# Turning the second half's rows with VectorE and a round trip through DRAM in a spectral filter plus GEGLU kernel

## Chip, cores and metric

One core of a Trainium2 chip runs the whole kernel. The metric is the device time of one execution in microseconds, median over runs. TensorE (PE), VectorE (DVE), ScalarE (ACT) and GpSimd (POOL) each work through their own list of instructions in order; SyncE (SP) issues DMA transfers from a queue of its own, also in order.

## The reference

```python
def _A_ref(x, w_r, w_i):                      # x: 1 x 2048 x 512
    X = rfft2(x, axes=(-2, -1))
    X = X * (w_r + 1j * w_i)                  # 2048 x 257
    return irfft2(X, s=(S, D), axes=(-2, -1))
def _B_ref(x, w_gate, w_up, w_down):          # 512 -> 1376 -> 512
    return (gelu(x @ w_gate) * (x @ w_up)) @ w_down
h = x + _A_ref(layernorm(x), w_r, w_i)        # layernorm: eps 1e-5, no scale or shift
h2 = h + _B_ref(layernorm(h), w_gate, w_up, w_down)
```

Everything is float32. The gelu is the tanh approximation.

## The kernel before

The rows are 16 blocks of 128 (block b), the 512 columns four chunks of 128. Both Fourier transforms are matrix products. The MLP has 11 blocks f of 128 hidden columns; the rows of blocks 0 to 7 are the first half, 8 to 15 the second, and a **tile** t{n} is one hidden block for one half: t0 to t10 for the first half, t11 to t21 for the second. Every float32 operand of the MLP stands as two parts, a high and a low one (fp32r), and a product of two operands is three matmuls. A tile computes gate and up with seven products P0 to P6 over combinations of the operand's quarters in place of eight; a product is six matmuls of 128x512. The seven combinations of the rows stand in `cb`, those of the weights in `gu`.

The order of work is written out by hand. Strings of tokens (`START`, `SECOND`, `FIRST`, `FIRST_HALF`, `SECOND_HALF`) list steps; each step gives its instructions to its engines in the order of the string. SyncE's transfers and some other things are placed by the scheduler. The strings, in order of time:

- `START`: statistics and roots of layer norm (s, r, n), sums of rows (f, u, v), and for each b the transform over rows (a, b) until some 31 us.
- `SECOND`: over d (o), the filter (f), back (b), with p and h as preparations.
- `FIRST`: the way back of the first eight blocks, their second layer norm, their turning (T) and combinations, and the first tiles.
- `FIRST_HALF`: tiles t2 to t10 and all that makes the second half's rows. Its tokens: t{n}P0 to P6 the products; t{n}c1 to c3 copies by ScalarE out of PSUM; d1, d2, dy the sums of products and m0, m1, o0, o1 the end of a tile, on VectorE; G0, G1 gelu; i0, i1 rounding of the result. y{n}.k is a step on the weights of tile n: raw loads by SyncE, differences by GpSimd, rounding to the high part by ScalarE, low part by GpSimd (t10's are y10). D{g}{i}@k is the down projection of group g of tiles for row block i into PSUM bank k; E{g}{i} adds that bank to `gh` and so gives it back. For the last group D30 and D31 are begun without their last tile, and F30, F31 do that third (three matmuls). N0, N1 are inverse roots of the second half's variances, each two Newton chains of short operations; S0 (`keep_rows`) writes scales and means of the second half's rows to DRAM, for `rescale` and `means` to spread them later.

The part that the change touches most: a normalised row block of 128x512 must stand with its columns on the partitions before TensorE can use it as `cb`. For the second half, `turned(i, banks)` works on block 8 + i (h = 0) and 12 + i (h = 1). H{i}{h} normalises on ScalarE. T0 and T1 transpose four 128x128 pieces each by TensorE against `ident` into a PSUM bank (lines 596 and 602). Then a, b make high and low part of combinations 0 and 1; s, z, e are copies by ScalarE into SBUF; c, d, h, k are the differences, f, g / i, j, n, o / l, m high and low part of the others. All of this comes late in `FIRST_HALF`, after t9's products; i{i}x is step x of pair i. The copies s and z also put the turned rows into `gh` (`ht`), where the second half keeps its residual.

Of the kernel before, what the change touches and what calls it, by code (L numbers as in the profile page):

```python
# [51 lines left out]
u4.0 w4 u0.1 C4.0 w0 C0.1 U1.2 C1.4 U5.3 C5.5 V4.2 X4 V0.3 X0 M4.1 O4.0 V1.0 M0.2 O0.1 X1 r0 V5.1 X5 H4 G4 H0 I4 U2.3  # L52
C2.5 V2.3 M5.1 U7.2 H5 C7.1 S4 O5.0 G0 A4 g0awh I0 S0 A0 M1.3 O1.1 Q0 U3.4 E0.5 V7.4 X2 C3.5 U6.0 C6.0 N0 R01 I5 R00
H1 G5 S5 X7 M2.1 V6.3 H2 G1 I1 S1 X6 U8.4 C8 T01.2 s0.0 O2.1 l0 T00 A5 A1 c0 V3.1 Q1 M7.0 O7.0 E1.6 U9.7 a0 N1 R10
M6.4 T10 X3 I2 d0 e0.1 k0 H7 H6 f0 g0 b0 h0 U12.3 G2 R11 T11.1 a1 I7 M3.2 C12 U15.3 b1 g0aP0 s1.2 c1 i0 G7 O3.1 O6.0
U10.4 n0 H3 d1 j0 S7 C15 C9 e1.0 g1aP0 h1 m0 k1 n1 C10 f1 l1 I3 G3 S3 I6 A7 U14.5 A3 g1 G6 g1aP1 g0ac1 g0aP2 g0aP3 Q3
g0awl g1ac1 g1aP2 C14 o0 E3.7 N3 o1 i1 m1 R31 T31.5 S2 g0ac2 A2 S6 A6 R30 Q2 r1 s3.6 E2.6 N2 j1 g0aP4 T30 c3 g0aP1 d3
g1ac2 g1aP4 g0ac3 g0aP5 R20 T20 g0ad1 a3 b3 e3.4 h3 k3 g1ac3 g1aP5 r2 f3 R21 g0ady g0aP6 g3 g1aP3 i3 j3 T21.7 a2 b2
g0bP0 g0aG0 g1ad1 g1ady K9.5 g0ad2 g0bP1 s2.8 n3 c2 d2 g1bP0 g1aP6 K12.4 g1bP1 g0bc1 g0bd1 r3 l2 f2 g2 g0bP2 g0aG1
g0am1 g1bc1 g1bP2 g1aG0 e2.7 k2 n2 g1ad2 o3 g0bc2 h2 o2 m2 l3 i2 g0am0 g0bG0 g1bd1 g0bP3 g1bc2 g0bP4 g0ai1 g1aG1 j2  # L60
g0bc3 g0bdy g1bP4 g1bP3 g0ai0 g1bc3 g1awh g0bP5 m3 g1am0 g0bP6 K8.4 lo1 g1ai0 g1bdy g1bG0 g1bP6 g0ao0 g1ao0 g0ao1
# [85 lines left out]
def kernel(  # L147
# [508 lines left out]
    def in_turn(i, hns, banks):  # L656

        do = combine(i, hns)
        places = {"T0": ps[:, banks[0]], "T1": ps[:, banks[1]], "s": ht[:, 1, :, i], "z": ht[:, 0, :, i], "e": row()}
        for names in ("T0 a b z", "T1 s c d e f g h k", "i j l m n o"):  # L660
            for k in names.split():
                do[k](*[places[k]] if k in places else [])
            yield
# [782 lines left out]
```

## Time and profile before

| | |
|---|---|
| time, median of 3 runs | 437.88 us (437.83 to 438.65) |
| profiled execution: span from first to last instruction | 436.2 us |
| TensorE busy | 429.6 us (98%), 2283 matmuls |
| VectorE busy | 303.7 us (70%) |
| ScalarE busy | 262.3 us (60%) |
| GpSimd busy | 326.4 us (75%) |
| DMA moved | 41.61 MB, mean 95 GB/s |

The profiled execution has no time of its own beside the span; the median of the runs is 1.7 us above the span, which is what lies before the first and after the last instruction, or between executions. A share of busy time is an average over stages; the rows further down are from single stages. TensorE's granted clock is at its full level, 2.4 GHz, in every slice of the page.

### The profile page before, as it was taken

The page shows a single profiled execution, that of the slowest core. Times are in us where ns is not written, and L with a number is a line of the kernel's source. Part 1 is how long each engine was busy: PE and PEld are TensorE (multiplying, and loading weights), DVE is VectorE, ACT ScalarE, POOL GpSimd, SP SyncE. Part 2 cuts the span into 40 slices and gives each one's busy share as a digit, 9 for nine tenths or more (in the row PEclk, how much of TensorE's full clock was granted, in tenths as well). Part 3 has the DMA queues.
Part 4 walks back from the last instruction along what each step waited for, and adds up shares of the span by engine and source line. Part 5 has one row for each costly group of instructions (what it writes and reads, how often), then busy time and mean ns, then how long its engine had stood idle before and what let it go on. Part 6 is the DMA issues. An engine that isn't in the chain of part 4 may idle for free.

```text
span 436.2 us, 6671 instructions
## 1 busy us (share of the span) xinstructions
PE 429.6 (98%) x2283; PEld 368.6 (84%) x2283; DVE 303.7 (70%) x570; ACT 262.3 (60%) x536; POOL 326.4 (75%) x355
## 2 busy tenths in 40 slices
...
GB/s 286 402 414 85 379 23 144 106 50 24 2 121 122 73 49 98 72 25 72 72 11 63 98 50 120 146 46 28 72 49 73 54 44 57 65 26 0 1 2 194
DMA packets 23543, 41.61 MB, mean 95 GB/s; under 512 B 4178, under 2 KB 9810, under 8 KB 23380
## 3 DMA queue, kind: packets, MB, share of 16 engines
...
q14 instruction: 17, 0.14, 0.1%
...
## 4 chain that ended last, share of the span: by engine, by line
PE 92%; DMA 4%; POOL 1%; DVE 1%; issue 1%; ACT 0%; SPq 0%; DVEq 0%; POOLq 0%
PE ps L192 16%; PE ps L190 16%; PE ps L191 16%; PE ps L1241 14%; PE ps L1034 11%; DMA gh<-in_x 4%; PE ps L454 3%; PE ps L563 3%; PE ps L469 3%; PE ps L496 3%; PE ps L826 2%; PE ps L1212 1%; POOL pn L368 1%; PE ps L1142 1%; PE ps L596 1%; PE ps L602 1%
## 5 line engine op out<-in xcount | busy, mean ns | idle before, releaser
L190 PE MATMUL ps<-cb,gu 128*128 128x512 f32 (+1 forms) x336 | 125.8, 375 | 0.0
L192 PE MATMUL ps<-cb,gu 128*128 128x512 f32 (+1 forms) x336 | 124.9, 372 | 0.0
L191 PE MATMUL ps<-cb,gu 128*128 128x512 f32 (+1 forms) x336 | 124.8, 371 | 0.0
L706 ACT ACTIVATE s<-ps 128x512 f32<-128x512 f32 (+1 forms) x72 | 40.3, 561 | 56.7 <-PE ps L192 56.4
L257 POOL TENSOR_TENSOR gu<-raw,gu 128x768 fp32r<-128x768 f32 (+1 forms) x42 | 61.6, 1483 | 16.7 <-ACT gu L254 14.7
L190 PEld LDWEIGHTS ps<-cb,gu 128*128 128x128 f32 x336 | 63.3, 188 | 11.0 <-ACT s L706 0.2
L192 PEld LDWEIGHTS ps<-cb,gu 128*128 128x128 f32 x336 | 63.2, 188 | 11.0
L191 PEld LDWEIGHTS ps<-cb,gu 128*128 128x128 f32 x336 | 63.3, 188 | 10.9
L1241 PE MATMUL ps<-wd,a 128*128 128x512 f32 x264 | 63.4, 390 | 0.0
L1241 PEld LDWEIGHTS ps<-wd,a 128*128 128x128 f32 x264 | 49.3, 188 | 10.1
L712 ACT ACTIVATE s<-s 128x512 f32<-128x512 f32 (+1 forms) x48 | 28.4, 593 | 33.5 <-DVE s L709 33.3
L715 DVE TENSOR_TENSOR ps<-ps,s 128x512 f32<-128x512 f32 (+1 forms) x48 | 30.9, 651 | 22.5 <-PE ps L192 19.9
L1041 DVE TENSOR_TENSOR gh<-ps,gh 128x512 f32<-128x512 f32 x66 | 44.2, 681 | 0.8 <-PE ps L1034 0.8
L709 DVE TENSOR_TENSOR s<-ps,s 128x512 f32<-128x512 f32 (+1 forms) x48 | 30.7, 641 | 17.2 <-PE ps L192 15.8
L254 ACT ACTIVATE gu<-raw 128x768 fp32r<-128x768 f32 (+1 forms) x42 | 28.6, 698 | 4.9 <-POOL raw L240 4.6
L1253 DVE TENSOR_TENSOR gh<-ps,gh 128x512 f32<-128x512 f32 x24 | 16.4, 686 | 19.8 <-PE ps L1241 19.8
L709 DVE TENSOR_TENSOR ps<-ps,s 128x512 f32<-128x512 f32 (+1 forms) x24 | 15.6, 652 | 17.0 <-ACT s L706 14.5
L544 POOL TENSOR_TENSOR wd<-wdr,wd 128x512 fp32r<-128x512 f32 x12 | 15.5, 1295 | 13.9 <-ACT wd L542 13.9
L234 POOL TENSOR_TENSOR raw<-raw 128x256 f32<-128x256 f32 x16 | 11.8, 737 | 17.2 <-DMA raw<-in_wgu 15.5
L947 POOL TENSOR_TENSOR t<-mis,t 128x768 fp32r<-128x768 f32 (+1 forms) x9 | 13.3, 1481 | 14.1 <-ACT t L945 14.0
L728 DVE TENSOR_TENSOR a<-ps,a 128x512 fp32r<-128x512 f32 (+1 forms) x26 | 15.1, 603 | 10.8 <-ACT a L721 10.5
L485 POOL TENSOR_TENSOR z<-t,t 128x520 f32<-128x520 f32 x15 | 19.4, 1295 | 2.7 <-DVE t L477 2.1
...
## 6 DMA issues: line engine op xcount, KB each, us to landing
...
raw<-in_wgu SPq DMA_DIRECT2D x32, 256.0 KB, 3.1
out<-gh SPq DMA_DIRECT2D x15, 256.0 KB, 2.0
...
row<-in_x SPq DMA_DIRECT2D x12, 256.0 KB, 3.6
wdr<-in_wd SPq DMA_DIRECT2D x12, 256.0 KB, 2.7
mis<-in_wd SPq DMA_DIRECT2D x10, 256.0 KB, 2.6
a<-in_wgu SPq DMA_DIRECT2D x8, 256.0 KB, 3.5
```

The lines of the kernel that those rows point to most:

```text
L190: pe.matmul(o, lh, rh, start=(i == 0 and not onto), stop=False, skip_group_check=True)
L191: pe.matmul(o, lh, rl, start=False, stop=False, skip_group_check=True)
L192: last = pe.matmul(o, ll, rh, start=False, stop=(i == n - 1), skip_group_check=True)
L254: by.activation(r[:, 0, m], t[:, m], AF.Copy)
L257: pooled["lo"] = pool.tensor_tensor(r[:, 1, m], t[:, m], r[:, 0, m].bitcast(F32), op=ALU.subtract)
L706: return lambda: act.activation(to, a, AF.Copy)
L709: return lambda: dve.tensor_tensor(to, a, b, op=ALU.add)
L712: return lambda: act.activation(g, g, AF.Gelu_apprx_tanh)
L715: return lambda: dve.tensor_tensor(u, u, g, op=ALU.mult)
L1034: pe.matmul(ps[:, k], w[:, hw], a[ha], start=start and hw + ha == 0, stop=hw == 1, skip_group_check=True)
L1041: by.tensor_tensor(to, o, to, op=ALU.add)
L1241: pe.matmul(o, a[:, ha, i // 4, rows_of], wds[f][:, hw], start=start, stop=stop)
```

## The change

The 32 TensorE transposes of the second half go. `turned(h)` now lets VectorE transpose each normalised block, 128x512, into a tile `t`: J{i}{h}. VectorE turns pieces of 32x32 only, so the pieces still lie in the wrong partitions. When the four blocks of a half h are there, J{h} (`leave`) writes `t` to DRAM (`across`) in four transfers of 256 KB, one for each 32 partitions, and reads it back into `gh` in one of 1 MB: ten transfers for both halves. `combined(i, banks)` then makes the combinations out of `gh`: s, z, e are not needed, i and j now take two combinations in one step, b and m stand on GpSimd. Rows come out in another order within a half, which is undone when the output is taken apart. `keep_rows` turns scales and means with one small VectorE transpose, too, and writes them with four transfers of rows of 128 bytes, in place of two of single words. In `FIRST_HALF` the tokens of all this stand elsewhere, and `START`, `SECOND` and `FIRST` list the same steps in another order. The matmuls of START, SECOND and FIRST are the same in number.

```diff
 START = """
-f0 s0 g0 r0 n0 s1 c0 v0 g1 s2 m3 q3 r1 g2 f1 v1 n1 r2 m5 c1 q5 n2 c2 m7 c3 f2 s4 s6 g4 a0 b0 w7 g6 v2 q7 r4 n4 m9 c4
...
+s0 g0 r0 n0 s1 c0 m3 q3 f0 v0 g1 s2 r1 g2 r2 m5 f1 n1 v1 c1 q5 n2 c2 c3 f2 v2 s4 s6 g4 g6 m7 q7 r4 n4 a0 b0 w7 m9 c4
...
 FIRST_HALF = """
...
-i0T1 Z0 w9.2 i1z t10c2 t10P4 i0a i0b i0s i0c t10P3 i0d t10d1 t10c3 t10dy i0z i0e i0h Z1 i0f i0g w10.0 w10.1 t10P5 i0i
-E32 D34@6 i1e i1k i2e i2k i1h i2n i3e i2b i3k i3n E33 i2o i1n i1o i3a i3b D35@7 i2f i2h i3m i3h E34 D36@6 i1l i1m i3o
+t7m1 E21 D23@7 E20 D22@6 t8dy t8P6 t7i1 t7o1 H31 J31 H01 J01 E22 t8d2 t9P1 t8G0 H11 J11 H21 J21 t8P5 D24@6 w8.0 E23
+t10i0 t10o0 D31@7 i2h D30@6 F30 E30 i2k t10i1 t10o1 i2f i2g i2i i2j i1h i3c F31 E31 D32@6 i3k E32 D34@6 i3d i3f i1l
+i1g i2l i2m i3h i3i i1k i3j i3g E34 D33@7 D36@6 E33 i1i i1j D35@7 E35 D37@7 i3l i3m i1m i0l E36 i0m E37
...
         def rescale():
             for r in range(2):
-                at = kept_rows[0][4 * r : 4 * r + 4].rearrange("b n -> (b n)")
+                at = kept_rows[r].rearrange("q i n -> (q i n)")
                 spreading = nc.sync.dma_start(spread, at.partition_broadcast(P))
                 if not r:
...
-                nc.sync.dma_start(m[:1], kept_rows[1][4 * k : 4 * k + 4].rearrange("(o b) n -> o (b n)", o=1))
+                nc.sync.dma_start(m[:1], kept_rows[2 + k : 3 + k].rearrange("o q i n -> o (q i n)"))
...
-    kept_rows = [dram.tile([NB // 2, P], F32, name=f"rows{i}") for i in range(2)]
+    kept_rows = dram.tile([4, 4, 4, 32], F32, name="rows")
...
     def keep_rows():
-        sd = w3.tile([P, NB // 2], F32, name="sd", bufs=1)
-        dve.scalar_tensor_tensor(sd, mv2[:, NB // 2 :, 1], EPS, rs2[:, NB // 2 :], op0=ALU.add, op1=ALU.mult)
-        for to, a in zip(kept_rows, (sd, mv[:, NB // 2 :, 0])):
-            nc.sync.dma_start(to.rearrange("b n -> n b"), a)
-    def turned(i, banks):
-        hn = [None, None]
-        def normed(h):
-            hn[h], b = row(), 8 + i + 4 * h
-            act.activation(hn[h], gh[:, b], AF.Copy, scale=rs2[:, b : b + 1])
-        for h in range(2):
-            later[f"H{i}{h}"] = functools.partial(normed, h)
-        ops = combine(i, hn)
-        places = {"T0": ps[:, banks[0]], "T1": ps[:, banks[1]], "s": ht[:, 1, :, i], "z": ht[:, 0, :, i]}
-        for k in "T0 a b z T1 s c d e f g h k i j l m n o".split():
-            if k == "e":
-                later[f"i{i}e"] = lambda: ops["e"](row())
-            elif k in places:
-                later[f"i{i}{k}"] = functools.partial(ops[k], places[k])
-            else:
-                later[f"i{i}{k}"] = ops[k]
+        sd, st = (w3.tile([P, 32], F32, name=n, bufs=1) for n in ("sd", "st"))
+        dve.memset(sd, 0.0)
+        dve.scalar_tensor_tensor(sd[:, :8], mv2[:, NB // 2 :, 1], EPS, rs2[:, NB // 2 :], op0=ALU.add, op1=ALU.mult)
+        dve.tensor_copy(sd[:, 8:16], mv[:, NB // 2 :, 0])
+        dve.transpose(st, sd)
+        for q in range(4):
+            nc.sync.dma_start(kept_rows[:, q].rearrange("k i n -> k i n"), st[32 * q : 32 * q + 16])
+    def turned(h):
+        tr, hns = None, {}
+        def normed(i):
+            hns[i], b = row(), 8 + i + 4 * h
+            act.activation(hns[i], gh[:, b], AF.Copy, scale=rs2[:, b : b + 1])
+        def turn(i):
+            nonlocal tr
+            if tr is None:
+                tr = w3.tile([P, 16, 4, 32], F32, name="t", bufs=1)
+            dve.transpose(tr[:, :, i], hns[i])
+        def leave():
+            for q in range(4):
+                at = slice(32 * q, 32 * q + 32)
+                to = across[h].rearrange("(j r) n -> r j n", r=32)[:, :, q * P : (q + 1) * P]
+                nc.sync.dma_start(to, tr[at].rearrange("r j i n -> r j (i n)"))
+            nc.sync.dma_start(htf[:, h], across[h].rearrange("(c p) n -> p c n", p=P))
+        for i in range(4):
+            later[f"H{i}{h}"] = functools.partial(normed, i)
+            later[f"J{i}{h}"] = functools.partial(turn, i)
+        later[f"J{h}"] = leave
+    def combined(i, banks):
+        hi, lo = cb[:, 0, :, :, i], cb[:, 1, :, :, i]
+        a0, a1, s0, s1 = (ht[:, h, c : c + 2, i] for h in range(2) for c in (0, 2))
+        w = [ps[:, k].rearrange("p (m c n) -> p m c n", m=2, c=2) for k in banks]
+        def less(to, a, b, eng=dve):
+            return lambda: eng.tensor_tensor(to, a, b, op=ALU.subtract)
+        def high(m, a):
+            return lambda: act.activation(hi[:, m], a, AF.Copy)
+        def low(m, a, eng=dve):
+            return lambda: eng.tensor_tensor(lo[:, m], a, hi[:, m].bitcast(F32), op=ALU.subtract)
+        first = ht[:, 0, :, i].rearrange("p (m c) n -> p m c n", c=2)
+        ops = {
+            "a": high(slice(0, 2), first),
+            "b": low(slice(0, 2), first, pool),
+            "c": less(w[0][:, 0], s0, a0),
+            "d": less(w[0][:, 1], s1, w[0][:, 0]),
+            "f": high(slice(3, 5), w[0]),
+            "g": low(slice(3, 5), w[0]),
+            "h": less(w[1][:, 1], a1, w[0][:, 1]),
+            "k": less(w[1][:, 0], s1, s0),
+            "i": high(slice(5, 7), w[1]),
+            "j": low(slice(5, 7), w[1]),
+            "l": high(2, s1),
+            "m": low(2, s1, pool),
+        }
+        for k in ops:
+            later[f"i{i}{k}"] = ops[k]
+    across = [dram.tile([D, 4 * P], F32, name=f"across{h}") for h in range(2)]
+    for h in range(2):
+        turned(h)
...
     for i, banks in enumerate(((3, 4), (5, 0), (3, 4), (1, 2))):
-        turned(i, banks)
+        combined(i, banks)
...
-    y[:, NB // 2 :, ORDER] = second.reshape(D, NB // 2, P).transpose(2, 1, 0)
+    y[:, NB // 2 :, ORDER] = second.reshape(D, 2, 4, 4, 32).transpose(2, 4, 1, 3, 0).reshape(P, NB // 2, D)
```

Three places of the program, as the engines' lists stand in it. The first is SyncE's queue while the second half's rows are made: `raw<-in_wgu` are loads of weights, `rows` and `dis` carry the scales (S0 and the spread of `rescale`), `wdr` the down weights. Before:

```order
L538 DMA wdr<-in_wd 128x512
L1264 DMA rows_925<-sd 128x8x1
L227 DMA raw<-in_wgu 128x512
L228 DMA raw<-in_wgu 128x2x256
L1059 DMA dis<-rows_925 128x512
L538 DMA wdr<-in_wd 128x512
L227 DMA raw<-in_wgu 128x512
```

After, from the load of down weights ahead of S0 on:

```order
L537 DMA wdr<-in_wd 128x512
L1257 DMA rows<-st 4x4x32 x4
L1280 DMA across_926<-t 32x16x128 x4
L226 DMA raw<-in_wgu 128x512
L227 DMA raw<-in_wgu 128x2x256
L1281 DMA gh<-across_926 128x4x512
L1049 DMA dis<-rows 128x512
L1280 DMA across_927<-t 32x16x128 x4
L1281 DMA gh<-across_927 128x4x512
L537 DMA wdr<-in_wd 128x512
```

The one scatter of scales gave way to four transfers; the four writes of the first half h and their reading back stand ahead of the spread `dis<-rows`, those of the second behind it, and so behind the wait of that spread for GpSimd's first step on tile ten's weights.

The second place is TensorE behind tile ten's last product: L1241 and L1231 are the down projection (D30 and so on, nine matmuls each, F30 and F31 three), L596 and L602 the transposes, L190 to L192 and L189 to L191 products of tiles. Before:

```order
L192 MATMUL ps<-cb,gu 128x512
L1241 MATMUL ps<-wd,a 128x512 x12
L602 MATMUL ps<-ident,row 128x128 x4
L1241 MATMUL ps<-wd,a 128x512 x3
L602 MATMUL ps<-ident,row 128x128 x8
L596 MATMUL ps<-ident,row 128x128 x4
L1241 MATMUL ps<-wd,a 128x512 x3
L596 MATMUL ps<-ident,row 128x128 x4
L1241 MATMUL ps<-wd,a 128x512 x54
```

After:

```order
L191 MATMUL ps<-cb,gu 128x512
L1231 MATMUL ps<-wd,a 128x512 x27
L189 MATMUL ps<-cb,gu 128x512
L190 MATMUL ps<-cb,gu 128x512
L191 MATMUL ps<-cb,gu 128x512
...
L190 MATMUL ps<-cb,gu 128x512
L191 MATMUL ps<-cb,gu 128x512
L1231 MATMUL ps<-wd,a 128x512 x18
L189 MATMUL ps<-cb,gu 128x512
L190 MATMUL ps<-cb,gu 128x512
L191 MATMUL ps<-cb,gu 128x512
```

Before, the transposes stood between the pieces of D30 to F31, and then 54 matmuls of down projection came in a row. Now D31, D30 and F30, F31 and D32 are 27 matmuls without a break, and two products of tile eleven, 12 matmuls, stand between D32 and D34.

The third place is VectorE at the same time: L709/L699, L715/L705 and L728/L718 are d2 and m, o and j of tile ten, L1250/L1240 the sums E3i, L618/L1295 the differences c, d, h, k and L624/L1301 the low parts. Before:

```order
L709 TENSOR_TENSOR s_2464<-ps,s_2464 128x512
L715 TENSOR_TENSOR ps<-ps,s_2463 128x512
L715 TENSOR_TENSOR ps<-ps,s_2464 128x512
L728 TENSOR_TENSOR a<-ps,a 128x512
L624 TENSOR_TENSOR cb<-ps,cb 128x4x128
L728 TENSOR_TENSOR a<-ps,a 128x512
L1250 SCALAR_TENSOR_TENSOR gh<-ps,mv,gh 128x512
L618 TENSOR_TENSOR ps<-gh,ps 128x256 x3
L1250 SCALAR_TENSOR_TENSOR gh<-ps,mv,gh 128x512
L618 TENSOR_TENSOR ps<-gh,ps 128x256 x3
L1250 SCALAR_TENSOR_TENSOR gh<-ps,mv,gh 128x512
L618 TENSOR_TENSOR ps<-ps,row 128x256
```

After:

```order
L718 TENSOR_TENSOR a<-ps,a 128x512
L1295 TENSOR_TENSOR ps<-gh,ps 128x256
L1240 SCALAR_TENSOR_TENSOR gh<-ps,mv,gh 128x512
L1295 TENSOR_TENSOR ps<-gh 128x256
L718 TENSOR_TENSOR a<-ps,a 128x512
L1301 TENSOR_TENSOR cb<-ps,cb 128x4x128 x2
L1295 TENSOR_TENSOR ps<-gh,ps 128x256
L1295 TENSOR_TENSOR ps<-gh 128x256
L1240 SCALAR_TENSOR_TENSOR gh<-ps,mv,gh 128x512
L1295 TENSOR_TENSOR ps<-gh 128x256
L1240 SCALAR_TENSOR_TENSOR gh<-ps,mv,gh 128x512
L1295 TENSOR_TENSOR ps<-gh,ps 128x256
```

The differences now read `gh` and not PSUM banks that TensorE had filled; three of them stand between E30 and the next sums, and the order of sums and low parts is another.

## Rows read from the trace of the kernel before

**Rows 1.** The page: busy time, share of the span and instructions of each engine.

```profile
PE 429.6 (98%) x2283; PEld 368.6 (84%) x2283; DVE 303.7 (70%) x570; ACT 262.3 (60%) x536; POOL 326.4 (75%) x355
```

**Rows 2.** Stretches: us, busy (instructions) of PE, PEld, DVE, ACT, POOL; PEclk, DMA share, GB/s.

```profile
238.00:255.00 17.00, 17.00 (x82) 13.96 (x81) 10.55 (x18) 11.94 (x23) 12.77 (x14) 1.00 0.19 63
255.00:262.00 7.00, 7.00 (x43) 6.00 (x42) 6.34 (x11) 5.62 (x13) 3.33 (x5) 1.00 0.20 76
262.00:274.00 12.00, 12.00 (x55) 9.92 (x54) 10.19 (x21) 5.79 (x17) 5.12 (x8) 1.00 0.34 119
300.00:430.00 130.00, 130.00 (x575) 107.63 (x574) 100.01 (x160) 70.96 (x125) 96.75 (x93) 1.00 0.14 45
```

**Rows 3.** The chain that ended last, pieces of it: start, duration, what.

```profile
220.91 4.08 PE ps L1241 x18
...
245.52 0.44 PE ps L596 x4
...
255.09 2.73 PE ps L1241 x12
...
258.26 0.70 PE ps L1241 x3
258.95 0.87 PE ps L602 x8
...
261.39 12.27 PE ps L1241 x54
```

**Rows 4.** Timeline of VectorE: start, duration, line, operation [idle before, releaser].

```profile
215.46 0.16 DVE L576 SCALAR_TENSOR_TENSOR rs<-ps,rs 128x4 f32<-128x4 f32 x1
...
244.19 0.69 DVE L709 TENSOR_TENSOR s<-ps,s 128x512 f32<-128x512 f32 x1 [1.36 <-PE ps L192]
...
262.06 1.09 DVE L618 TENSOR_TENSOR ps<-gh,ps 128x256 f32<-128x256 f32 x3
...
277.09 2.47 DVE L1064 TENSOR_TENSOR gh<-gh,ps 128x512 f32<-128x512 f32 x4
```

**Rows 5.** Groups of VectorE from 240 to 275 us: the sums E3.

```profile
L1250 DVE SCALAR_TENSOR_TENSOR gh<-ps,mv,gh 128x512 f32<-128x512 f32 x8 | 6.0, 750 | 1.8 <-PE ps L1241 1.7
```

**Rows 6.** DMA issues: count, KB each, median us from issue to landing.

```profile
raw<-in_wgu SPq DMA_DIRECT2D x32, 256.0 KB, 3.1
out<-gh SPq DMA_DIRECT2D x15, 256.0 KB, 2.0
...
mis<-in_mi SPq DMA_DIRECT2D x1, 1024.0 KB, 9.5
...
rows<-sd SPq DMA_DIRECT2D x1, 4.0 KB, 10.8
```

**Rows 7.** Timeline of GpSimd, the weights of tile ten.

```profile
233.69 0.74 POOL L234 TENSOR_TENSOR raw<-raw 128x256 f32<-128x256 f32 x1 [11.51 <-DMA raw<-in_wgu]
...
241.51 1.86 POOL L257 TENSOR_TENSOR gu<-raw,gu 128x768 fp32r<-128x768 f32 x1 [0.86 <-ACT gu L254]
```

**Rows 8.** Timeline of ScalarE, tile ten's last rounding and its copy c1.

```profile
240.60 0.84 ACT L254 ACTIVATE gu<-raw 128x768 fp32r<-128x768 f32 x1
...
242.89 0.60 ACT L706 ACTIVATE s<-ps 128x512 f32<-128x512 f32 x1 [1.45 <-PE ps L192]
```

**Rows 9.** Timeline of TensorE and of VectorE near the end of the first stage.

```profile
26.10 0.61 PE L401 MATMUL ps<-ms,uv 128*128 128x128 f32 x4
26.90 0.68 PE L401 MATMUL ps<-ms,us 128*128 128x128 f32 x4 [0.19 <-DVE us L388]
27.42 0.61 PE L401 MATMUL ps<-ms,uv 128*128 128x128 f32 x4
27.87 0.61 PE L401 MATMUL ps<-ms,us 128*128 128x128 f32 x4
...
25.81 1.41 DVE L388 TENSOR_TENSOR us<-pn 128x256 f32<-128x256 f32 x2
```

More of the change, by code (lines that the diff above doesn't have):

```diff
@@ L36 @@
 START = """
-f0 s0 g0 r0 n0 s1 c0 v0 g1 s2 m3 q3 r1 g2 f1 v1 n1 r2 m5 c1 q5 n2 c2 m7 c3 f2 s4 s6 g4 a0 b0 w7 g6 v2 q7 r4 n4 m9 c4
-s8 c5 c6 q9 a1 a2 b1 a3 f4 f6 m11 b2 k0 v4 s10 q11 g10 g8 c7 v6 b3 a4 f8 a5 b5 b4 r8 k2 k1 n8 c8 s12 f10 a6 m13 c9 c10
-c11 k4 a7 b7 f12 f14 q13 s15 v8 g12 s14 k3 b6 k7 g15 a8 a9 k5 g14 r12 v10 n12 b8 v12 b9 k9 c12 a11 u13 c13 a10 b10 u14
-k8 f15 b11 a12 b12 k6 a13 k10 c14 c15 k11 v14 u15 b13 k13 k12 v15 a14 b14 a15 b15 z4 l15 k14 k15
+s0 g0 r0 n0 s1 c0 m3 q3 f0 v0 g1 s2 r1 g2 r2 m5 f1 n1 v1 c1 q5 n2 c2 c3 f2 v2 s4 s6 g4 g6 m7 q7 r4 n4 a0 b0 w7 m9 c4
+s8 c6 c5 q9 a1 b1 a3 f4 f6 m11 b2 k0 v4 s10 q11 g10 c7 v6 g8 r8 k1 a2 k2 n8 c8 b3 a4 f8 a5 b5 b4 s12 f10 a6 m13 c9 k4
+q13 c11 c10 f14 a7 b7 f12 v8 g12 s14 b6 k7 k3 s15 g15 a8 a9 k5 g14 v10 r12 n12 b8 v12 b9 k9 c12 a11 u13 c13 a10 b10
+u14 k8 b11 a12 b12 k6 k11 v14 b13 a13 c14 k10 c15 k12 k13 f15 v15 a14 b14 u15 a15 l15 b15 z4 k14 k15
 """
@@ L51 @@
 FIRST = """
[L52 to L61, printed above, removed]
@@ L84 @@
-L15 t7P3 R15 t7P4 t6d2 y8.4 y8.5 y8.6 y8.7 y8.8 y8.9 y8.10 t7c3 t6o0 t7dy t6G1 t6m1 t8P0 t8c1 B14.1 t7G0 t6i1 B11.1
-t7P5 t7m0 t7i0 t8P2 B15.0 w7.0 y9.0 y9.1 w7.1 t7P6 t8P3 w7.2 y9.2 y9.3 t6o1 t7o0 t8c2 y9.4 y9.5 B15.1 N0 N1 t8P4 t8c3
-H00 H01 H10 t8P1 H11 y9.6 t7d2 t7G1 y9.7 y9.8 y9.9 D21@7 D20@6 t9P0 E21 D23@7 E20 D22@6 S0 t8d1 t8G0 t7m1 t7i1 t7o1
-t9P1 y9.10 y10.0 t8P5 t9c1 t9d1 t9P2 H20 H21 E22 y10.1 t8dy D24@6 t8P6 w8.0 E23 D25@7 y10.2 H30 t8d2 y10.3 E24 D26@6
-t8m0 H31 t8G1 t8m1 y10.4 y10.5 y10.6 y10.7 y10.8 E25 D27@7 t8i0 E27 t9c2 w8.1 w8.2 t9P4 t9G0 t8i1 t9P3 t9c3 w9.0 y10.9
```

46 lines of the change are left out of this document (26 added, 20 removed).

## The prediction

> **What bounds the kernel now.** I read the page's busy line first, then the chain that ended last, then busy time by stretch. TensorE is busy for 429.6 of 436.2 us [rows 1], and in all four stretches that matter here, from 238 us on, it is busy for the whole stretch [rows 2]. The chain of work that ended last is there an unbroken run of matmuls [rows 3]: no other engine releases any of them. So a microsecond of TensorE work taken out is worth a microsecond, as long as TensorE finds its next operands ready. VectorE is the next fullest: 6.3 of 7 us and 10.2 of 12 us in the stretches from 255 to 274 us [rows 2], which is where the change adds VectorE work and takes TensorE work away.
>
> **What is removed.** The second half's rows are turned by 32 TensorE transposes, eight groups of four. One group takes 0.44 us in the chain, a double one 0.87 us [rows 3]: 8 x 0.44 = 3.5 us, all of it on the path. Twelve copies on ScalarE (s, z, e) go too; ScalarE has 5.8 busy us in the 12 from 262 us [rows 2], so they are worth nothing by themselves. **Removed: 3.5 us.**
>
> **The turning by VectorE.** Eight transposes of 128x512, SBUF to SBUF. The trace has none. Below, four back-to-back 128x512 operations take 2.47 us, 0.62 us apiece [rows 4]; above, the dearest row of that size on any engine that could do it is GpSimd's 768-wide one at 1.86 us [rows 7], which for 512 columns is about 1.25 us. I take 0.6 to 0.7 us, since every VectorE row of this width lies there. In the changed order five stand just behind the two chains of short operations on the variances, which ended at 215.6 us [rows 4], before the sums E21 and E20 that give back banks 7 and 6. Behind 215.6 us come the five (3.25 us), tile seven's m1 (0.62 us) and E21 (0.75 us [rows 5]): E21 ends near 220.3 us. Its bank is wanted by D23, which with D22 begins at 220.91 us in the chain [rows 3] and has one product more ahead of it now, 222.3 us. At 1.25 us each, E21 would end near 223.2 us and cost 0.9 us.
>
> The row of TensorE says 0.44 us per 128x512 on an engine without idle time [rows 3]. The Trainium skill, "DVE Perf Modes", section "Rules for kernel authors", speaks against the change: it gives a 128x128 transpose to TensorE wherever PSUM may be its target. By that rule there would be no gain, 437.9 us; by the row there is one, because VectorE's extra 5 us fall into its idle time and TensorE's 3.5 us did not.
>
> **The round trip.** Four writes of 256 KB and one read of 1 MB for each half. For the second: its last two transposes stand behind the sum E22 and tile eight's d2. The chain has D23 and D22 end at 220.91 + 4.08 = 224.99 us [rows 3]; the new order puts one product more ahead of them (1.36 us, six matmuls at 12.27/54 = 0.227 us [rows 3]) and tile eight's P6 after them: 227.7 us, and with d2 and two transposes 229.6 us. SyncE issues the four writes by 231 us. The stated landing of 256 KB is 2.0 us for a store [rows 6]: the four land at 233 us if they overlap, at 239 us if each waits for the last. The read of 1 MB lies between a 256 KB load at 3.1 us and the 1 MB of mis at 9.5 us [rows 6]: back at 236 to 248.5 us, and I take 241 us. The first reader is i1c, on VectorE right behind tile nine's d2, which starts at 244.19 us in the profile [rows 4] and moves by little: 244.9 us. Covered by 4 us in the middle, late by 3.6 us at the worst end. SyncE's queue has the spread of the scales ahead of these writes, waiting for GpSimd's first step on tile ten's weights; that step came at 233.69 us, 11.5 us late, behind the scatter of 4-byte words rows<-sd that took 10.8 us to land [rows 6, 7]. But for that it could have come at 222.2 us. The scatter is gone; I put the step at 227 us, between, and expect no wait for it at 229.6 us.
>
> **Terms that cost.** Let T be the end of tile ten's last product, 255.09 us in the chain [rows 3].
>
> (1) Weights of tile ten. Its last rounding (0.84 us, at 240.60 us [rows 8]) moves on ScalarE behind the copy c1 of the same tile, which starts at 242.89 us [rows 8]. So it ends near 242.89 + 0.60 + 0.84 = 244.33 us, and GpSimd's low half (1.86 us [rows 7]) at 246.2 us. P2 now stands where a transpose group began, at 245.52 us [rows 3], and its third matmul, the first to read the low half, two matmuls later, at 245.97 us: **0.25 us**.
>
> (2) F30. After T the order on VectorE is d2, j of row group 0, m1, o0; m1 waits for a gelu, which I take at the 0.60 us of ScalarE's copy of that width [rows 8]. With steps of 0.6 us on VectorE [rows 4]: d2 to 0.75, j to 1.35, m1 1.45 to 2.05, o0 to 2.75 us. Before, F30 came at 258.26 us, T + 3.17 [rows 3], with a transpose group as filler; now it could start 12 x 0.227 = 2.73 us after T. Nearly even if VectorE is punctual at T, up to 0.4 us if its list from i1c on (in which I count 0.9 us without work, by the same steps) is a little late: 0.2 us.
>
> (3) D32 into bank 6 now has only F31 (0.68 us) between it and F30, which wrote that bank. The sum E30 must come between: it takes 0.75 us [rows 5], and I allow 0.1 us for the handing over. So D32 waits 0.85 - 0.68 = 0.17 us with VectorE standing ready, more if it comes late: 0.3 us. Together (2) and (3): **0.5 us**, from 0 to 0.9.
>
> (4) D34 is written by hand right behind D32 in the same bank, and its release E32 is the tenth operation on VectorE after E30: i2k, i1h, i3c, i3k at 0.36 us (three in 1.09 us [rows 4]), o1, g and j at 0.6 us, E31 and E32 at 0.66 us (0.75 us less an overlap with the neighbour, as the four in 2.47 us have it), 4.6 us, so T + 9.1 us. By itself that is 2.4 us of wait. The order that the program really has puts P0 and P1 of the next tile between (2.72 us): D34 comes at T + 9.5 us. **Costed at nothing**; the cover is 0.4 us, and beyond it every microsecond of VectorE's lateness is one of TensorE's. The same holds for D37 behind D35, with P4 and another product as cover.
>
> (5) The start. Pair 13's matmuls wait for a sum on VectorE at 26.90 us: that group of four starts 0.80 us after the one ahead, where the next two start 0.45 us apart, so 0.35 us [rows 9]; there b13 now stands ahead of a13 and fills this. But the last fold on VectorE now stands behind v14, and u15 behind v15, so a15 waits for one operation more, 0.7 us (two in 1.41 us [rows 9]), with b14 to cover part of it. Net **+0.15 us**, from -0.35 (nothing new) to +0.4 us. Filter and way back keep their matmul order almost unchanged: 0, within 0.2 us.
>
> **Sum.** -3.5 + 0.25 + 0.5 + 0.15 = -2.6 us: span 436.2 to 433.6 us. The timed median is 437.88 us, 1.7 us above the span, which I leave as it is: **435.3 us**. From 300 to 430 us TensorE is full and VectorE has 30 us idle [rows 2], so I expect nothing new there.
>
> **Rivals.** (a) The forecast, 434.4 to 436.4 us: chance 0.50. (b) VectorE is late in the tail by 1 to 2.5 us more than I list, so that D34, D32 and F30 all wait: 436.4 to 437.6 us. For it: VectorE is 85 to 91% busy from 255 to 274 us [rows 2] and dependent short operations may take longer than my steps. Against it: two products stand in as cover. 0.20. (c) No wait at all and the start's 0.35 us regained: 437.88 - 3.5 - 0.35 = 434.0 us. 0.15. (d) The other side: the second round trip comes back late. It decides from the point where i1c waits more than about 3.5 us, that is a landing after 248.4 us; then VectorE, in order, holds up m0 of tile nine, everything of tile ten, F30 and D32. At the worst end of both ranges and with another 2 us of queueing, i1c waits 5.6 us, less 0.9 us of slack, less 2.6 us: 440 us. For it: 10.8 us once for a small transfer [rows 6]. Against it: no comparable load on the queues then. 0.10. (e) The change does not do what it says: TensorE's 3.5 us are there as waits at other places, as the skill's rule would have it, about 437.9 us: 0.05.
>
> A measurement of this kernel tells a difference of 0.2% (0.9 us) from none, so faster means below 437.0 us: (a), (c) and half of (b), 0.75; within: half of (b) and (e), 0.15; slower: 0.10. The range 434.0 to 437.6 us holds (a), (b), (c), and leaves out most of (d).
>
> **What would show it.** Right: no matmuls with ident after 120 us; TensorE busy 3.5 us less after 200 us; the store of t to landing under 5 us and gh<-across under 7 us; VectorE's first 128x256 subtraction from gh not waiting for a DMA; gaps on TensorE only before F30 and D32, each below 0.4 us. Wrong: transposes of 1.2 us; a DMA as releaser of that subtraction; a gap before D34 or D37; TensorE waiting for GpSimd at tile ten's P2 by more than 0.5 us. A wait in the first 75 us that the profile of before does not have would break term (5), the one that I worked out most roughly.

## The result, and the profile after

The change made the kernel slower: 439.95 us against 437.86 us for the kernel before on the same chip, ratio 1.0044 (95% interval 1.0031 to 1.0058). The forecast was 435.3 us. The profiled execution has a span of 438.5 us, 2.3 us more than before. (Some executions of kernels with the new START fell into a slower state at a lower clock; ratios leave them out, here and below.)

What was to go, went: no matmul with `ident` is left behind 120 us. The page, as [rows 1]:

```profile
PE 428.7 (98%) x2251; PEld 364.7 (83%) x2251; DVE 310.7 (71%) x581; ACT 258.4 (59%) x520; POOL 327.0 (75%) x351
```

32 matmuls fewer, 0.9 us less busy time, and a longer span: TensorE waits more. The waits of TensorE in the changed kernel (engine, line, what it waited for: us in all, times, longest), of which the kernel before has only the first and, with 0.2 us, the `us` one:

```profile
PE ps L200 <- POOL ident masks.py:199: 1.4, 1, 1.4
PE ps L400 <- ACT ms L358: 1.0, 2, 0.7
PE ps L1231 <- DVE gh L1240: 0.8, 2, 0.7
PE ps L468 <- DVE t L476: 0.5, 1, 0.5
PE ps L400 <- POOL pn L367: 0.5, 1, 0.5
PE ps L189 <- DVE ps L699: 0.4, 1, 0.4
...
PE ps L400 <- DVE us L387: 0.2, 1, 0.2
PE ps L816 <- DVE a L826: 0.2, 1, 0.2
```

They lie at two ends. Lines 400, 468 and 816 are START, SECOND and FIRST, where the change turns no row; lines 189 and 1231 are the tail behind tile ten. To see what each stage costs I read five marks off TensorE's timeline: the first matmul over d (SECOND begins), the first of the way back (FIRST), the first down projection, the first down projection of the second half (line 1034 before, 1024 after; products of tiles eleven and twelve lie ahead of it), and the end of the last matmul. In us, with all later kernels, and their ratios to the kernel before, which ran beside each. The later kernels ran on three other chips, where the kernel before took 439.1 us and not 437.86 us, so they are compared by ratio:

| kernel | over d | way back | down | second half | last | span | ratio (95%) |
|---|---|---|---|---|---|---|---|
| before | 30.12 | 73.63 | 129.53 | 292.55 | 431.46 | 436.2 | |
| after | 31.57 | 76.26 | 133.17 | 295.67 | 434.58 | 438.5 | 1.0044 (1.0031 to 1.0058) |
| after_again | 31.19 | 75.90 | 132.42 | 294.85 | 433.76 | 437.7 | 1.0013 (1.0003 to 1.0022) |
| new_lists | 31.47 | 76.15 | 132.63 | 296.99 | 435.90 | 440.5 | 1.0071 (1.0056 to 1.0085) |
| old_lists | 29.89 | 73.39 | 129.28 | 291.47 | 430.38 | 434.3 | 0.9933 (0.9919 to 0.9947) |
| old_start | 30.25 | 74.94 | 131.73 | 294.50 | 433.41 | 437.3 | 0.9985 (0.9977 to 0.9994) |
| new_first | 30.06 | 73.56 | 130.04 | 292.20 | 431.11 | 435.0 | 0.9950 (0.9936 to 0.9964) |
| second_fix | 30.35 | 74.20 | 130.72 | 292.92 | 431.83 | 435.8 | 0.9958 (0.9945 to 0.9970) |
| start_fix | 30.91 | 75.63 | 132.30 | 294.76 | 433.67 | 437.6 | 1.0010 (0.9998 to 1.0021) |
| start_fix2 | 30.54 | 75.21 | 131.89 | 294.31 | 433.22 | 437.1 | 0.9995 (0.9986 to 1.0005) |
| one_sbuf | 29.99 | 73.49 | 129.38 | 292.48 | 431.38 | 435.3 | 0.9961 (0.9949 to 0.9973) |
| one_sbuf2 | 29.87 | 73.38 | 129.27 | 290.25 | 429.16 | 433.1 | 0.9911 (0.9897 to 0.9925) |
| rows_only | 29.91 | 73.41 | 129.30 | 292.69 | 431.60 | 435.8 | 0.9968 (0.9956 to 0.9981) |
| before_again | 29.91 | 73.41 | 129.99 | 293.95 | 432.86 | 437.5 | 1.0005 (0.9995 to 1.0015) |

Of the changed kernel, the lag behind before is 1.45 us at the start of SECOND, 2.63 us at that of FIRST, 3.64 us at the first down projection, and 3.12 us from the second half's first down projection on. So the loss is made ahead of the tail, and the tail gives back only some 0.5 us of the 3.5 us that were taken out of it.

**The tail.** VectorE's eight subtractions c and k, whose two operands both stand in `gh`, that is in SBUF, are long; those of d and h, with one operand in PSUM, are not. VectorE's timeline:

```profile
248.60 1.52 DVE L1295 TENSOR_TENSOR ps<-gh 128x256 f32<-128x256 f32 x1
...
252.21 0.43 DVE L1295 TENSOR_TENSOR ps<-gh 128x256 f32<-128x256 f32 x1
252.55 0.42 DVE L1295 TENSOR_TENSOR ps<-gh,ps 128x256 f32<-128x256 f32 x1
...
253.60 1.02 DVE L1295 TENSOR_TENSOR ps<-gh 128x256 f32<-128x256 f32 x1
```

and GpSimd's at the same time:

```profile
247.99 1.85 POOL L256 TENSOR_TENSOR gu<-raw,gu 128x768 fp32r<-128x768 f32 x1 [0.93 <-ACT gu L253]
249.79 1.49 POOL L543 TENSOR_TENSOR wd<-wdr,wd 128x512 fp32r<-128x512 f32 x1
253.02 1.31 POOL L1301 TENSOR_TENSOR cb<-gh,cb 128x512 fp32r<-128x512 f32 x1 [1.74 <-ACT cb L1298]
```

The first began at 248.60 us under a GpSimd instruction that ended at 249.84 us, and ended 0.28 us after it; the one of 253.60 us ended at 254.62 us, 0.29 us after GpSimd's of 253.02 us. At 252.21 us GpSimd stood idle and the same subtraction took 0.43 us. So it is with all eight: the seven that begin under a GpSimd instruction take 0.59 to 1.52 us and end 0.29 us behind the end of that one, in one case of the next. Behind them TensorE waits for VectorE; its timeline, tile ten's P6, D32 and D34:

```profile
256.78 0.50 PE L189 MATMUL ps<-cb,gu 128*128 128x512 f32 x1 [0.42 <-DVE ps L699]
...
263.31 2.33 PE L1231 MATMUL ps<-wd,a 128*128 128x512 f32 x9 [0.15 <-DVE gh L1240]
...
269.02 4.37 PE L1231 MATMUL ps<-wd,a 128*128 128x512 f32 x18 [0.65 <-DVE gh L1240]
```

### The profile page after: what moved, and what is told of

It reads as the page before. It is cut to its first block, busy times and chain, and to the rows that moved or that the text cites. A ratio compares the mean times of both kernels' runs of the same rounds, so it can differ in the third digit from the quotient of the medians.

```text
span 438.5 us, 6613 instructions
## 1 busy us (share of the span) xinstructions
PE 428.7 (98%) x2251; PEld 364.7 (83%) x2251; DVE 310.7 (71%) x581; ACT 258.4 (59%) x520; POOL 327.0 (75%) x351
## 4 chain that ended last, share of the span: by engine, by line
PE 78%; POOL 4%; DVE 3%; ACT 3%; DMA 1%; issue 1%; DVEq 0%; POOLq 0%
PE ps L189 15%; PE ps L190 15%; PE ps L191 15%; PE ps L1231 12%; PE ps L1024 11%; PE ps L495 3%; PE ps L468 2%; PE ps L453 2%; POOL gh L830 2%; PE ps L562 1%; PE ps L1202 1%; DMA wdr<-in_wd 1%; PE ps L1132 1%; DVE ps L1295 1%; POOL row L834 1%
## 5 line engine op out<-in xcount | busy, mean ns | idle before, releaser
L189 PE MATMUL ps<-cb,gu 128*128 128x512 f32 (+1 forms) x336 | 125.7, 374 | 0.6 <-DVE ps L699 0.4
L190 PE MATMUL ps<-cb,gu 128*128 128x512 f32 (+1 forms) x336 | 124.8, 371 | 0.0
L191 PE MATMUL ps<-cb,gu 128*128 128x512 f32 (+1 forms) x336 | 124.8, 371 | 0.0
L189 PEld LDWEIGHTS ps<-cb,gu 128*128 128x128 f32 x336 | 63.3, 188 | 12.6 <-DVE ps L699 1.0
L191 PEld LDWEIGHTS ps<-cb,gu 128*128 128x128 f32 x336 | 63.3, 188 | 11.1
L190 PEld LDWEIGHTS ps<-cb,gu 128*128 128x128 f32 x336 | 63.3, 188 | 10.7
L1231 PE MATMUL ps<-wd,a 128*128 128x512 f32 x264 | 64.1, 391 | 0.9 <-DVE gh L1240 0.8
L1231 PEld LDWEIGHTS ps<-wd,a 128*128 128x128 f32 x264 | 49.2, 188 | 12.7 <-DVE gh L1240 1.7
L705 DVE TENSOR_TENSOR ps<-ps,s 128x512 f32<-128x512 f32 (+1 forms) x48 | 30.8, 651 | 23.4 <-PE ps L191 21.2
L699 DVE TENSOR_TENSOR s<-ps,s 128x512 f32<-128x512 f32 (+1 forms) x48 | 30.5, 638 | 6.9 <-PE ps L191 6.2
L699 DVE TENSOR_TENSOR ps<-ps,s 128x512 f32<-128x512 f32 (+1 forms) x24 | 15.6, 650 | 10.3 <-ACT s L696 9.3
L718 DVE TENSOR_TENSOR a<-ps,a 128x512 fp32r<-128x512 f32 (+1 forms) x26 | 15.3, 602 | 9.3 <-ACT a L711 8.8
L460 ACT ACTIVATE dp<-ps 64x512 f32<-64x512 f32 x30 | 17.7, 591 | 6.2 <-PE ps L453 6.0
```

Of the source, the lines that this page charges most:

```text
L189: pe.matmul(o, lh, rh, start=(i == 0 and not onto), stop=False, skip_group_check=True)
L190: pe.matmul(o, lh, rl, start=False, stop=False, skip_group_check=True)
L191: last = pe.matmul(o, ll, rh, start=False, stop=(i == n - 1), skip_group_check=True)
L699: return lambda: dve.tensor_tensor(to, a, b, op=ALU.add)
L705: return lambda: dve.tensor_tensor(u, u, g, op=ALU.mult)
L1231: pe.matmul(o, a[:, ha, i // 4, rows_of], wds[f][:, hw], start=start, stop=stop)
```

## Experiments

**Which lists lose.** Two kernels cross the lists with the turning, and one takes START alone:

```diff
 new_lists: before.py with
+START, SECOND, FIRST of after.py
 old_lists: after.py with
+START, SECOND, FIRST of before.py
 old_start: after.py with
+START of before.py
```

> The kernel before, with the lists START, SECOND and FIRST of the changed kernel; the second half's rows are turned by TensorE as before. In the two traces TensorE's first matmul of SECOND came 1.45 us later after the change, the first of FIRST 2.63 us later and the first down projection 3.64 us later. Theory A, the new orders cost this: 440.5 to 441.7 us, with the same three lags. Theory B, the first loads of x merely landed later in that one execution (ScalarE waited for one until 7.58 us, before until 6.91 us), and the lists are worth little, as the prediction had it: 437.7 to 438.6 us.

> The changed kernel with START, SECOND and FIRST of the kernel before: the turning, the round trip and the new order of FIRST_HALF alone. Theory A: the loss of the first 130 us goes, and what is left is the gain of the second half that the traces show, a lag of 3.80 us at 203 us that became 3.12 us at 292 us: 436.2 to 437.4 us. Theory B: 439 us or more, since the loss then lies elsewhere. The prediction's own sum for this kernel is 435.1 us.

> The changed kernel with only START taken from the kernel before. Theory A with START at 1.45 us of the loss: 438.3 to 438.8 us. If START carries nearly all of it and the later lags are its echo: 436.3 to 437.3 us. If SECOND or FIRST carry it: 439.5 us or more.

Theory A, but not in every number. The three new lists alone make the kernel before 0.71% slower, with nearly the lags of the changed kernel at the first marks (1.35, 2.52 and 3.10 us); the changed kernel with the old lists is 0.67% faster than before, 2.9 us. The times that were expected stood against the first chip's 437.86 us. On that scale the ratios are 441.0 us for new_lists, inside theory A's range; 434.9 us for old_lists, faster than its range; and 437.2 us for old_start, in the range of "START carries nearly all". The marks speak against that last reading: old_start begins SECOND early and still takes 44.69 us for it, as the changed kernel does, where old_lists takes 43.50 us. From after_again, run on a later chip, to old_lists it is 0.80%, 3.5 us. START carries 0.28% of this (after_again against old_start). The landing of the first loads does differ from run to run (ScalarE's wait for x is 0.2 us in before, 0.7 us in old_start, 1.0 us in after), but old_start with 0.7 us begins SECOND only 0.13 us later than before.

> The changed kernel with START and SECOND of before, so old_lists with FIRST as changed. second_fix (new FIRST, SECOND new but for two tokens) stands 0.25% over old_lists. If FIRST carries that: 0.995 to 0.9965 of the kernel before, and TensorE's waits stand at the first of FIRST's back products, at line 816 and at tile one's first products (0.36, 0.3 and 0.23 us in old_start). If it is the rest of SECOND: 0.9925 to 0.994.

```diff
 new_first: after.py with
+START, SECOND of before.py
```

FIRST carries 0.17% (against old_lists), at the edge of the range expected; the intervals of the two overlap, so this share is the least sure. It leaves 0.35%, 1.5 us, for SECOND (old_start against new_first). Of the places that were expected only the 0.23 us at tile one's products is there; from the first way back to the first down projection it is 56.48 us against 55.89 us in old_lists. Where the other 0.4 us lie I did not resolve. (In before_again, which has the old FIRST, this stretch is 56.58 us, for one wait that is shown under the scatter below; in the five other traces with the old FIRST it is 55.89 or 55.90 us.)

**Two tokens of SECOND.**

> Built on old_start (new SECOND and FIRST), with two tokens of SECOND put back: f2 behind o4 on TensorE again, p3 ahead of both. In old_start f2's matmuls waited 0.71 us at 36.34 us for the bank that VectorE was reading for f0, where o4 stood before, and VectorE waited 0.61 us at 41.11 us for ScalarE's p3. Theory F, these two tokens carry SECOND's loss: from the first matmul of SECOND to the first of FIRST 43.5 to 43.7 us as with the old list, and not 44.7 us, and the time 0.7 to 1.2 us under old_start. Rival: VectorE's filter is the bound all along, and the gap moves to a later f: within 0.3 us.

```diff
 SECOND = """
-p0 h o0.6 o1.0 h h o2.2 p4 f0 p1 f1 p2 o3.0 h f2 o4.2 o5.0 p3 f3 h p6 ...
+p0 h o0.6 o1.0 h h o2.2 p4 f0 p1 f1 p2 o3.0 h p3 o4.2 f2 o5.0 f3 h p6 ...
```

Theory F: 0.27% under old_start, 1.2 us, and 43.85 us from over d to the way back against 44.69 us, where 43.5 to 43.7 us was expected. So the two tokens carry most of SECOND's loss, and 0.35 us of the stretch stay with the rest of the list. TensorE in old_start, lines 453 the over-d product and 468 the filter:

```profile
34.74 1.05 PE L453 MATMUL ps<-dfs,ts 128*128 128x128 f32 x8
36.34 1.10 PE L468 MATMUL ps<-dp,cfs 128*128 128x256 f32 x4 [0.55 <-DVE t L476]
```

and in second_fix:

```profile
34.83 1.95 PE L453 MATMUL ps<-dfs,ts 128*128 128x128 f32 x16
36.62 1.03 PE L468 MATMUL ps<-dp,cfs 128*128 128x256 f32 x4
```

Eight over-d matmuls more stand ahead of f2, while VectorE reads f0's bank (its last operation on it, L476, runs from 35.50 us for 0.69 us in old_start). The wait is gone, and no later one takes its place at full size.

**The end of START.**

> The changed kernel with two tokens of START exchanged, f12 and f14, which stand as before again; it moves two pairs of GpSimd's folds and nothing else. In the changed kernel the last fold of GpSimd is 512 wide and ends at 26.53 us, and TensorE has a gap of 0.66 us at 26.58 us behind it and VectorE one of 1.84 us. Theory S, that exchange makes this gap: the first matmul of SECOND comes 0.5 to 0.8 us earlier than in the changed kernel and the time falls by as much. Rival: ScalarE's later statistics (gaps of 0.90 and 0.45 us at 10.59 and 15.13 us) set the end of START: less than 0.2 us.

```diff
-q13 c11 c10 f14 a7 b7 f12 v8 g12 s14 ...
+q13 c11 c10 f12 a7 b7 f14 v8 g12 s14 ...
```

Theory S fails: the gap at 26.58 us is gone, SECOND begins 0.28 us earlier than in after_again, and the time is the same as after_again. TensorE in the changed kernel, line 400 the transform over rows:

```profile
26.58 1.16 PE L400 MATMUL ps<-ms,pn 128*128 128x128 f32 x8 [0.49 <-POOL pn L367]
...
30.18 0.68 PE L400 MATMUL ps<-ms,us 128*128 128x128 f32 x4 [0.20 <-DVE us L387]
```

and in start_fix, where the gap stands behind the last sums:

```profile
29.52 0.68 PE L400 MATMUL ps<-ms,us 128*128 128x128 f32 x4 [0.64 <-ACT ts L408]
```

(The releaser named is ScalarE's `ts`; the order puts VectorE's last sum, u15, there as well.) So the next kernel puts the last sums back too:

> start_fix with the end of START put back too: f15 three steps ahead, u15 behind u14 and ahead of v15, b13 ahead of a13. In start_fix the gap of 0.66 us at 26.58 us was gone and a gap of 0.80 us stood at 29.52 us instead, TensorE waiting for VectorE's u15, so the loss had only moved to the next late sum. Theory S2, GpSimd's and VectorE's last sums together set the end of START: the first matmul of SECOND comes 0.5 to 1.0 us earlier than in start_fix, and the ratio goes from 1.0010 to 0.998 to 0.9995. Rival, the order of the first statistics sets it: as start_fix within 0.1%.

```diff
-u14 k8 b11 a12 b12 k6 k11 v14 b13 a13 c14 k10 c15 k12 k13 f15 v15 a14 b14 u15 a15 ...
+u14 k8 f15 b11 a12 b12 k6 k11 v14 u15 b13 a13 c14 k10 c15 k12 k13 v15 a14 b14 a15 ...
```

0.15% under start_fix (the intervals overlap) and 0.18% under after_again: the ratio is at the upper edge of what S2 gave, and SECOND begins 0.37 us earlier than in start_fix, less than the 0.5 us expected. About two thirds of START's 0.28% lie in these last sums, together with b13 and a13 that moved with them; the rest lies ahead of them and was not taken apart.

> The changed kernel once more, as a mark for the three runs beside it on this chip: 0.4 to 0.6% over the kernel before.

It came out at 1.0013, under what was expected. Why is the subject of the last two runs.

**Two operands in SBUF.** Built on old_lists:

```diff
-"c": less(w[0][:, 0], s0, a0),
+"p": lambda: act.activation(w[0][:, 0], s0, AF.Copy),
+"c": less(w[0][:, 0], w[0][:, 0], a0),
...
-"k": less(w[1][:, 0], s1, s0),
+"q": lambda: act.activation(w[1][:, 0], s1, AF.Copy),
+"k": less(w[1][:, 0], w[1][:, 0], s0),
```

and the eight tokens p and q in FIRST_HALF, where some of the c and k move a few places to stand behind them.

> Built on old_lists. The eight subtractions c and k, whose two operands both stand in SBUF, get one of them out of PSUM: ScalarE first copies it to the place of the result (eight copies of 128x256 more on ScalarE). In the changed kernel these eight took 0.43 to 1.52 us, 7.1 us in all, and each long one ended 0.2 to 0.3 us after the GpSimd instruction ended that was running as it began; those with one operand in PSUM took 0.41 to 0.43 us. Theory P, such a subtraction waits for the whole GpSimd instruction: all eight come down to about 0.43 us, VectorE is earlier by some 3 us at its end of the tail, TensorE's waits before the down projections and the last products of tile ten go, and the time falls by 1 to 2 us against old_lists. Rival Q, VectorE's order and the banks set TensorE's waits, and the long subtractions are slack or waits for their data: within 0.4 us of old_lists.

The subtractions came down to 0.42 to 0.43 us, as P says, but the kernel is 0.28% slower than old_lists. One of ScalarE's new copies waited for VectorE (at 248.38 us, 0.92 us) and held up tile ten's c2 behind it. TensorE in one_sbuf:

```profile
249.34 0.50 PE L189 MATMUL ps<-cb,gu 128*128 128x512 f32 x1 [1.38 <-ACT s L696]
```

That is a fault of the experiment, so it was repeated with these tokens later in ScalarE's list:

```diff
-t9o0 i0p i1d i0c t10c2 t10P4 t9i1 t9o1 i0q ...
+t9o0 i1d t10c2 t10P4 t9i1 i0p t9o1 i0c i3a i3b t10c3 i0q ...
```

> one_sbuf with ScalarE's eight copies placed later in its list, so that tile ten's c2 and o don't wait behind them (in one_sbuf TensorE waited 1.54 us at 249.34 us for ScalarE's copy c2, which stood behind a copy that waited for VectorE). The subtractions take 0.42 to 0.43 us as in one_sbuf. Theory P: TensorE's waits from 244 us to 270 us, 2.3 us in old_lists, come down to 1 us or less, and the time is 0.8 to 1.8 us under old_lists (0.9915 to 0.989 of the kernel before). Rival: ScalarE's copies and their waits take the place of GpSimd's: 0.992 to 0.996.

0.9911: 0.22% or 1.0 us under old_lists, and the fastest of all. The second half's first down projection begins at 290.25 us against 291.47 us. The groups of VectorE from 244 to 272 us (busy us, mean ns), in old_lists:

```profile
L1295 DVE TENSOR_TENSOR ps<-gh 128x256 f32<-128x256 f32 x8 | 7.4, 931 | 0.1
...
L1295 DVE TENSOR_TENSOR ps<-gh,ps 128x256 f32<-128x256 f32 x8 | 3.3, 415 | 0.0
```

and in one_sbuf2:

```profile
L1296 DVE TENSOR_TENSOR ps<-ps,gh 128x256 f32<-128x256 f32 x8 | 3.4, 426 | 0.6 <-ACT ps L1314 0.5
L1296 DVE TENSOR_TENSOR ps<-gh,ps 128x256 f32<-128x256 f32 x8 | 3.4, 423 | 0.1
```

4.0 us of VectorE's time, and the waits of TensorE for its sums, 0.8 us in old_lists' waits from 244 us on, are gone. Not all gaps are. Let a gap be the time by which a matmul starts later than 0.227 us behind the one before it; the matmul at the gap then takes 0.11 us more itself. From 244 to 270 us the gaps are 2.2 us in old_lists and 1.25 us in one_sbuf2, where 1 us or less was expected: D34's is gone, and those at P6 (0.27 us), F30 (0.63 us) and D32 (0.32 us) stay. No run moves the tokens without moving the operands, so the 1.0 us belongs to both together; one_sbuf, with other places for them, shows the same 0.42 to 0.43 us.

**The scatter.**

> The kernel before with only keep_rows changed: scales and means turned by a small VectorE transpose and written in eight transfers of 128-byte rows, in place of two scatters of 4-byte words. The prediction: the scatter held up GpSimd's first step on tile ten's weights until 233.69 us, off TensorE's path; here that step comes 3 to 9 us earlier and the time stays within 0.1%. Rival: this is where the gain of the turning comes from, 0.2% or more faster.

```diff
 def keep_rows():                       # of before.py
...
+    dve.transpose(st, sd)              # scales in columns 0 to 7, means in 8 to 15
+    for q in range(4):
+        for k in range(2):
+            at = slice(32 * q + 8 * k, 32 * q + 8 * k + 8)
+            nc.sync.dma_start(kept_rows[k][:, 32 * q : 32 * q + 32], st[at])
```

> The kernel before, to have its trace from this chip too, since its median was 437.86 us on one chip and 439.1 us on two others. Ratio 1.000. If only the landing of the first loads differs: the first matmul of SECOND later than 30.12 us by as much as the span is longer, and all later marks of TensorE with it.

The rival: rows_only is 0.32% faster, 1.4 us, where the prediction had nothing. In the trace of before_again the scatter of the scales takes 12.6 us to land (10.8 us in [rows 6]) and GpSimd begins tile ten's weights at 235.52 us (233.69 us in [rows 7]):

```profile
235.52 0.74 POOL L234 TENSOR_TENSOR raw<-raw 128x256 f32<-128x256 f32 x1 [12.91 <-DMA raw<-in_wgu]
```

ScalarE rounds these weights when GpSimd has made their differences, and its next copy out of PSUM stands behind that. Its timeline in before_again:

```profile
237.93 0.85 ACT L254 ACTIVATE gu<-raw 128x768 fp32r<-128x768 f32 x1 [2.79 <-POOL raw L240]
...
239.16 0.59 ACT L706 ACTIVATE s<-ps 128x512 f32<-128x512 f32 x1
```

TensorE, which shows no such wait in the trace that the prediction had, stops for that copy ahead of its next product:

```profile
239.80 0.50 PE L190 MATMUL ps<-cb,gu 128*128 128x512 f32 x1 [0.78 <-ACT s L706]
```

new_lists has the same scatter, on another chip: 12.4 us to land, and

```profile
242.84 0.50 PE L190 MATMUL ps<-cb,gu 128*128 128x512 f32 x1 [0.99 <-ACT s L706]
```

In rows_only GpSimd begins 6.7 us earlier, and TensorE has no wait there:

```profile
228.79 0.74 POOL L234 TENSOR_TENSOR raw<-raw 128x256 f32<-128x256 f32 x1 [6.86 <-DMA raw<-in_wgu]
```

This wait is a third of the gain. The spans of before_again and rows_only are 1.7 us apart: 0.57 us of it lie between the first down projection and that of the second half, 0.69 us ahead of the former and 0.4 us behind the last matmul. By the traces what lies ahead goes back to the other scatter that rows_only takes out, that of the means, which SyncE issues at 30.46 us in before_again. From 34 to 44 us the DMA moves 29 GB/s there (80 in before, 177 in rows_only); a load of weights behind it in SyncE's queue comes late, and GpSimd waits for it, which it does in neither before nor rows_only:

```profile
53.90 0.73 POOL L234 TENSOR_TENSOR raw<-raw 128x256 f32<-128x256 f32 x1 [1.18 <-DMA raw<-in_wgu]
```

Behind that SyncE issues the next load of weights at 73.08 us (72.29 us in rows_only), when GpSimd has freed its place, and the reload of x behind it; VectorE starts on x at 79.41 us (78.56 us), and TensorE stops for VectorE's `a`:

```profile
80.30 1.10 PE L826 MATMUL ps<-row,mis 128*128 128x512 f32 x2 [0.44 <-DVE a L836]
```

No run takes out one scatter without the other, so the share of each is read from these two traces and not shown by a run. SECOND begins no later in before_again than in before, so the first loads are not it.

## Why the prediction was wrong

**The lists, the step that failed most.** "Filter and way back keep their matmul order almost unchanged: 0, within 0.2 us", and the start at +0.15 us, up to 0.4 us. They cost 3.5 us together: START 1.2 us, SECOND 1.5 us, FIRST 0.7 us, by the ratios. The sign that was to break term (5) was there: waits at 26.58 and 37.65 us that before does not have. In SECOND the matmul order was indeed almost unchanged, but o4, which changed places with f2, had been the cover for a bank that VectorE still reads, and this swap, with p3, cost 1.2 us. In START I named the right sums (the last fold, u15 behind v15) and put too little on them, and looked at no fold of GpSimd; the first part of START I did not look at. No rival had this loss as its mechanism; all bore on the second half.

**The turning** was right in what it removes. J took 0.65 us apiece, as I had it (four rows of two in 1.28 to 1.30 us); VectorE's timeline:

```profile
231.63 1.30 DVE L1273 STREAM_TRANSPOSE t<-row 128x512 f32<-128x512 f32 x2 [4.99 <-DMA across<-t]
...
234.03 1.28 DVE L1273 STREAM_TRANSPOSE t<-row 128x512 f32<-128x512 f32 x2
```

The wait of 4.99 us I had not seen: tile `t` has one buffer, and the second half's transposes wait until the first half's four writes have read it. TensorE has no wait there, so it cost nothing. The round trip, rival (d), came back in time: the first subtraction from `gh` does not wait for a DMA, though it begins 6.0 us after the second read was issued (242.57 us, 248.60 us); in one_sbuf ScalarE reads the second half's rows 6.4 us after the issue, without waiting for it. The eight writes took 4.6 us in the median, where "under 5 us" was to show the step right. GpSimd's first step on tile ten came at 233.32 us, not near 227 us: its load now stands behind the writes in SyncE's queue.

**The terms that cost.** Term (1), 0.25 us at tile ten's P2, is not there: its matmuls follow each other without a gap. A gap of 0.23 us stands two products on, at P4 (251.99 us), behind ScalarE's copy c2. Terms (2) to (4): I counted c and k at 0.36 us like the subtractions that [rows 4] show, all of which have one operand in PSUM; they took 0.89 us in the mean, 7.1 us for eight instead of 2.9 us. That is rival (b), VectorE late, by 4 us of work and not 1 to 2.5, and by a mechanism that I had not named. Three of the eight stand between E30 and E32 (the ninth operation behind E30, not the tenth) and took 2.5 us instead of 1.1 us: more than D34's cover of 0.4 us, so D34 got a gap of 0.81 us. P6 of tile ten got one of 0.58 us, F30 and D32 together 0.73 us. With P4's that is 2.35 us, and with the slower matmul at each of the six gaps 3.0 us, where 0.75 us was expected: 3.5 us less 3.0 us is the 0.5 us that the tail gave back. Terms (2) and (3), F30 and D32, were too low by themselves: their gaps stay in one_sbuf2, where no subtraction is long. The Trainium skill, "SBUF — State Buffer", section "Who interferes with whom", has a rule for this: a VectorE instruction with two SBUF inputs contends with a GpSimd instruction that reads SBUF, and the order of issue decides which of the two waits. The trace agrees, 0.43 us with GpSimd idle and up to 1.52 us behind it; one_sbuf and one_sbuf2 show that this, and not VectorE's order, made the subtractions long, and one_sbuf2 that it cost some 1.0 us.

**The sum.** By the ratios on the later chips: -0.32% for the two scatters, -0.35% for the turning (old_lists against rows_only), +0.80% for the lists, +0.13%, as after_again. For the scatters' part the trace of before on the first chip shows no wait; without it the sum is +0.45%, which is the 1.0044 measured there. That the scatters cost nothing on that chip is argued from one trace, not tried. The turning by itself gave 1.5 us (0.3 us of it behind the last matmul), against 2.75 us (the sum without the start), so rival (e), no gain from it at all, is out; one_sbuf2 gives back 1.0 of the 1.25 us that were missing. On the first chip the forecast of -2.6 us met +2.1 us, 4.7 us apart; by the ratios above, 3.35 us of that are the lists, which were put at 0.15 us, and 1.25 us the turning.

**Left open.** Behind the last matmul the span goes on for 4.7 us in before and before_again (4.6 us in new_lists, 4.2 us in rows_only) and for 3.9 us in every kernel with the turning; I did not find why. Nor did I take apart the first part of START or the 0.4 us of FIRST.
